# Moving the transpose of one bias out of a kernel's head, and settling its instruction order anew with a dearer table load

## The chip, the cores and the metric

The kernel runs on one core of a Trainium2 chip. The metric is device time in microseconds (us). The span that a profile reports is the time from the first to the last instruction; the device time is about 2 us longer.

Engines, as the profile names them: PE is TensorE's matmuls and PEld its weight loads, DVE is VectorE, ACT is ScalarE, POOL is GpSimd. SP only issues transfers here. PSUM has eight banks, in which PE leaves its results.

## The reference, cut to what matters

Two linear-attention blocks A and two feed-forward blocks B in turn, on 2048 tokens of width 512, with a LayerNorm before each and a residual sum after each.

```python
def _A_ref(x, wqkv, wo):
    q, k, v = split(x @ wqkv)                          # 32 heads of 16
    phi = lambda t: jnp.where(t > 0, t + 1, jnp.exp(t)) + 1e-6
    kv  = einsum(phi(k), v);  z = sum(phi(k))
    return (phi(q) @ kv) / (phi(q) @ z + 1e-6) @ wo
def _B_ref(x, w1, b1, w2, b2):
    h = gelu(layernorm(x) @ w1 + b1)                   # 512 -> 1792
    return h @ w2 + b2
x = x + _A_ref(layernorm(x), ...);  x = x + _B_ref(layernorm(x), ...)   # this line twice
```

The exponentials and logarithms of A and the Gelu of B need different ACT function tables, so ACT must load a table whenever it goes from one to the other.

## The kernel before

The kernel does not write its instructions in the order in which they run. It states a graph of operations. A small planner inside the program (a list scheduler) then simulates the engines with fixed costs, and from that settles, once and for all, the order on each engine and the PSUM bank of each tile. On the chip each engine follows its order strictly and waits on semaphores for what it needs. The planner's costs therefore cost no time on the chip; they only decide the order.

```python
SEM_LAT = 70.0
MM = 216.0
TABLE_LOAD = 1300.0        # what the planner thinks a table switch costs, in ns
...
                    if o.table is not None and table is not None and o.table != table:
                        at = max(o.ready, t0 + TABLE_LOAD)
                        pr += self.table_penalty
...
CONF = dict(N_HALF=1, N_K=4, ..., N_H=3, ..., TABLE_PENALTY=20.26, WINDOW=164.24,
            SHIFT={"B00_0": 1.5, "B00_1": -18.1, ...})   # priorities, found by search
```

`N_K` and `N_H` say how many PSUM banks the K products and the first feed-forward products may hold at once. `SHIFT` moves the priority of a group of operations.

The bias b1 (1792 numbers) is needed as a column for each block of 128. It is loaded as 14 rows, transposed by one small matmul and copied by ACT. In the kernel before that is planned ahead of everything but the warm-up matmuls:

```python
        b1b = Tile(psum, "b1", "g")
        G.op("pe", lambda e: e.matmul(bank(b1b)[:, 0:FT], lhsT=b1r[:, :], rhs=idp[0:FT, 0:FT], ...), 200,
             reads=["b1r", f"id{P}"], writes=["b1p"], tiles=[b1b], prio=-60, name="b1T", ...)
        G.op("act", lambda e: e.activation(b1c[:], bank(b1b)[:, 0:FT], ACT.Copy), 200, ..., prio=-60, name="b1c")
```

Two more operations: one is the LayerNorm of a tile of 128 tokens, whose inverse deviation comes from a chain of tiny POOL operations and which is then applied by DVE or ACT. The other is POOL's addition of b2 to the same tile:

```python
            G.op("dve", lambda e: e.tensor_scalar(yb[...], src(), mv[...], rstd[...],
                 op0=ALU.subtract, op1=ALU.mult), ..., name=f"norm{tag}", fast=True)
...
            G.op("pool", lambda e: e.tensor_tensor(xsb[:, st, :], xsb[:, st, :], b2b[:], op=ALU.add), 1120,
                 ..., prio=prio + 8, name=f"b2{L}_{st}")
```

## Time and profile before

| what | before |
|---|---|
| device time, median (range) | 344.92 us (344.75 to 345.35) |
| span of the profiled run | 343.1 us |
| PE, ACT, DVE, POOL busy | 96%, 72%, 58%, 31% |
| ACT table switches | 27, of 1283 ns each |
| first K matmul | at 10.04 us, waiting for its weights |

The first lines are from the page of before: busy time of each engine with its share of the span, and then the chain of work that ended last, by engine and by line.

```profile
PE 330.1 (96%) x1763; PEld 162.2 (47%) x1796; DVE 198.9 (58%) x430; ACT 247.6 (72%) x407; POOL 105.4 (31%) x199
...
PE 68%; ACT 12%; DVE 9%; POOL 5%; DMA 2%; issue 2%; ACTq 0%; DVEq 0%
...
L926 ACT ACT_TABLE_LOAD x27 | 34.6, 1283 | 0.5
```

PE is the limit, yet only 68% of the chain runs over PE. PE busy says little here, because the recorded matmuls overlap: one K product's matmul is recorded with a median of 379 ns, while in a stream the starts of full 128x512 matmuls are 216 ns apart. The spacing of the starts says more. I call every start that comes later than its predecessor's own time a stall.

These are PE's longest waits in before, from the waits view (what waited, for what, us in total, how often, longest; cut where dots stand):

```profile
PE ps L560 <- DVE yb L537: 1.6, 2, 1.0
...
PE ps L814 <- DMA b1r<-in_B_b_dram: 1.4, 1, 1.4
PE ps L599 <- DMA wqkv<-in_A_wqkv_dram: 1.1, 1, 1.1
PE ps L777 <- ACT t L570: 0.7, 1, 0.7
...
```

And this is the head in the timeline of before (start, duration, engine, line, operation, count, idle time before it and what ended it). L814 is the b1 matmul, L560 the transposes of the first tiles, L599 the first K product:

```profile
7.79 0.19 PE L814 MATMUL ps<-idp,b1r 14*128 14x14 bf16 x1 [1.41 <-DMA b1r<-in_B_b_dram]
7.91 1.03 PE L560 MATMUL ps<-idp,yb 128*128 128x128 bf16 x8
10.04 1.87 PE L599 MATMUL ps<-wqkv,t 128*128 128x512 bf16 x4 [1.09 <-DMA wqkv<-in_A_wqkv_dram]
```

PE waits 1.4 us for b1 and then does the transposes, but the K product behind them waits for its weights anyway.

### The profile page before, as it was taken

Reading aid. Unit: us, or ns where it says so; the run is one execution under the profiler, and the core shown is the slowest. Engines: PE = TensorE matmul, PEld = TensorE weight load, DVE = VectorE, ACT = ScalarE, POOL = GpSimd, SP = SyncE. Lnnn points to the kernel's source line nnn. Section 1 sums busy time; section 2 is a strip of 40 time slices with the busy share of each in tenths; the row PEclk is TensorE's granted clock in tenths of the full one; section 3 lists DMA queues with packets and bytes.
Section 4 is the critical chain, followed back from the end, with each engine's and each line's share of the span. In section 5 each row is a group of like instructions: output and inputs, shape, how many; then the busy total and the mean of one; then the engine's idle time right before and its main releaser. Section 6 shows DMA issues by size and latency. Waiting matters only on the chain.

```text
span 343.1 us, 4823 instructions
## 1 busy us (share of the span) xinstructions
PE 330.1 (96%) x1763; PEld 162.2 (47%) x1796; DVE 198.9 (58%) x430; ACT 247.6 (72%) x407; POOL 105.4 (31%) x199
## 2 busy tenths in 40 slices
PE   6899998999999999999999999998999999999996
PEld 2344453746544444444444454447744444444442
DVE  5588759759595343880375779989549218110122
ACT  1589669999979989968823399999995996527000
POOL 4662503526518031460022200054706604400000
PEclk9999999999999999999999999999999999999999
DMA  5832490004203020030011010000203301200011
GB/s 170 291 91 32 116 358 4 2 0 48 46 1 64 15 46 2 15 76 17 0 32 31 15 32 2 1 2 0 32 31 78 48 0 40 54 31 0 32 42 50
DMA packets 32116, 16.71 MB, mean 49 GB/s; under 512 B 26652, under 2 KB 30876, under 8 KB 32092
## 3 DMA queue, kind: packets, MB, share of 16 engines
q1 hardware_dynamic: 28876, 8.79, 12.6%
q0 software_dynamic: 1344, 5.77, 4.9%
q10 hardware_dynamic: 1872, 1.84, 1.6%
q8 instruction: 14, 0.23, 0.3%
q14 instruction: 10, 0.08, 0.1%
HBM read 8.00 MB, written 2.10 MB: 29 GB/s over the span
## 4 chain that ended last, share of the span: by engine, by line
PE 68%; ACT 12%; DVE 9%; POOL 5%; DMA 2%; issue 2%; ACTq 0%; DVEq 0%
PE ps L796 23%; PE ps L777 18%; PE ps L599 7%; PE ps L615 5%; PE ps L747 4%; ACT gT L783 4%; PE ps L680 4%; ACT L926 3%; PE ps L649 3%; DMA wqkv<-in_A_wqkv_dram 2%; DVE stats L513 2%; POOL xsb L763 2%; POOL rstd L525 2%; DVE xsb L752 2%; ACT eb L581 2%
## 5 line engine op out<-in xcount | busy, mean ns | idle before, releaser
L777 PE MATMUL ps<-t,w 128*128 128x512 bf16 (+1 forms) x555 | 102.0, 336 | 1.4 <-ACT t L570 0.7
L796 PE MATMUL ps<-w,gT 128*128 128x512 bf16 x441 | 101.4, 379 | 0.5
L783 ACT ACTIVATE gT<-ps,b1c 128x512 bf16<-128x512 f32 (+1 forms) x140 | 78.1, 605 | 21.4 <-PE ps L777 11.7
L777 PEld LDWEIGHTS ps<-t,w 128*128 128x128 bf16 x560 | 54.2, 98 | 45.8 <-ACT gT L783 2.1
L796 PEld LDWEIGHTS ps<-w,gT 128*128 128x128 bf16 x448 | 43.8, 98 | 52.2 <-ACT gT L783 0.5
L581 ACT ACTIVATE eb<-ps 128x512 bf16<-128x512 f32 x64 | 38.2, 598 | 22.6 <-PE ps L599 15.1
L763 POOL TENSOR_TENSOR xsb<-xsb,b2b 128x512 f32<-128x512 f32 x32 | 38.3, 1204 | 18.6 <-ACT yb L532 11.0
L585 DVE TENSOR_SCALAR eb<-eb 128x512 bf16<-128x512 bf16 x64 | 21.0, 329 | 39.4 <-ACT eb L581 39.4
L525 POOL TENSOR_TENSOR rstd<-veps,neghalf 128x1 f32<-128x1 f32 x64 | 37.2, 582 | 7.9 <-DVE veps L523 2.9
L583 ACT ACTIVATE rb<-ps 128x512 bf16<-128x512 f32 x64 | 38.4, 602 | 0.1
L734 DVE TENSOR_TENSOR t<-t,lr 128x512 bf16<-128x512 bf16 x32 | 22.4, 702 | 24.1 <-ACT lr L732 24.1
L806 DVE TENSOR_TENSOR outb<-ps,xsb 128x512 bf16<-128x512 f32 x16 | 11.1, 691 | 41.5 <-PE ps L796 41.5
L926 ACT ACT_TABLE_LOAD x27 | 34.6, 1283 | 0.5
L599 PE MATMUL ps<-wqkv,t 128*128 128x512 bf16 x124 | 32.6, 396 | 1.3 <-DMA wqkv<-in_A_wqkv_dram 1.1
L513 DVE BATCH_NORM_STATS2 stats<-xsb 128x6 f32<-128x512 f32 x48 | 32.8, 684 | 0.9
L747 PE MATMUL ps<-gtb,t 128*128 128x512 bf16 x124 | 31.5, 380 | 0.6 <-DVE t L734 0.2
L518 POOL TENSOR_SCALAR veps<-mv 128x1 f32<-128x1 f32 x32 | 6.3, 197 | 82.3 <-DVE mv L515 80.9
L615 PE MATMUL ps<-t,wqkv 128*128 128x512 bf16 x124 | 31.3, 379 | 0.2
L523 POOL TENSOR_SCALAR veps<-mv 128x1 f32<-128x1 f32 x29 | 8.1, 278 | 73.3 <-DVE mv L515 72.8
L532 ACT ACTIVATE yb<-xsb,nmr,rstd 128x512 bf16<-128x512 f32 x24 | 19.2, 809 | 13.1 <-PE ps L680 8.8
L537 DVE TENSOR_SCALAR yb<-xsb,mv,rstd 128x512 bf16<-128x512 f32 x24 | 18.4, 766 | 10.1 <-POOL rstd L525 9.7
L730 ACT ACTIVATE lr<-ps,eps 128x512 f32<-128x512 f32 x32 | 21.7, 679 | 1.7 <-PE ps L728 1.6
(59 smaller groups left out, 288.8 us busy)
## 6 DMA issues: line engine op xcount, KB each, us to landing
w<-in_B_w_dram POOLq DMA_DIRECT2D x4, 896.0 KB, 8.8
out_dram<-outb SPq DMA_DIRECT2D x16, 128.0 KB, 1.7
wqkv<-in_A_wqkv_dram ACTq DMA_DIRECT2D x2, 512.0 KB, 9.0
t<-in_A_x_dram POOLq DMA_DIRECT2D x2, 512.0 KB, 5.6
t<-yb SPq DMA_TRANSPOSE x48, 2.5
t<-in_A_x_dram ACTq DMA_DIRECT2D x1, 512.0 KB, 9.1
wqkv<-in_A_wqkv_dram POOLq DMA_DIRECT2D x1, 512.0 KB, 7.1
wo<-in_A_wo_dram POOLq DMA_DIRECT2D x1, 512.0 KB, 7.6
```

The lines of the kernel that those rows point to most:

```text
L513: G.op("dve", lambda e: e.bn_stats(stats[:, s.slot, :], src()), 620, reads=src_keys, writes=[k + "s"], tiles=[s, *src_tiles], prio=prio, n ...
L525: G.op("pool", lambda e: e.tensor_tensor(rstd[:, s.slot:s.slot + 1], veps[:, s.slot:s.slot + 1], neghalf[:], op=ALU.pow), 570, reads=[k + ...
L581: G.op("act", lambda e: e.activation(eb[:, et.slot, :], bank(bt), ACT.Exp), 478, reads=[src_key], writes=[f"e{tag}"], tiles=[bt, et], prio ...
L583: G.op("act", lambda e: e.activation(rb[:, rt.slot, :], bank(bt), ACT.Relu), 478, reads=[src_key], writes=[f"r{tag}"], tiles=[bt, rt], pri ...
L599: ins = e.matmul(bank(b), lhsT=yTa(yT)[:, dt, k * P:(k + 1) * P], rhs=wqkv[:, dt, D:2 * D], start=(dt == 0), stop=(dt == DT - 1))
L615: ins = e.matmul(bank(b), lhsT=wqkv[:, dt, kt * P:(kt + 1) * P], rhs=yTa(yT)[:, dt, :], start=(dt == 0), stop=(dt == DT - 1))
L747: ins = e.matmul(bank(wb), lhsT=yTa(pq)[:, kt, k * P:(k + 1) * P], rhs=gtb[:, kt, :], start=(kt == 0), stop=(kt == DT - 1))
L763: G.op("pool", lambda e: e.tensor_tensor(xsb[:, st, :], xsb[:, st, :], b2b[:], op=ALU.add), 1120, reads=[("x", st), "b2b"], writes=[("x", ...
L777: ins = e.matmul(bank(b, n), lhsT=w1[:, dt, ft * P:(ft + 1) * P], rhs=yTa(yT)[:, dt, k0 * P:k1 * P], start=(dt == 0), stop=(dt == DT - 1))
L783: G.op("act", lambda e, ft=ft, b=b, k0=k0, k1=k1, n=n: e.activation(gT[:, g.slot, ft * 512 + k0 * P:ft * 512 + k1 * P], bank(b, n), ACT.Ge ...
L796: ins = e.matmul(bank(b), lhsT=gT[:, g.slot, ft * 512 + k * P:ft * 512 + (k + 1) * P], rhs=w2[:, ft, :], start=(ft == 0), stop=(ft == FT - 1))
L926: e.preload_act_table_set(sets[table])
```

## The change

The intent: take b1's wait out of the head, and plan with 1420 ns for a table load instead of 1300, under which all the priorities were searched anew.

```diff
-TABLE_LOAD = 1300.0
+TABLE_LOAD = 1420.0
...
-    N_HALF=1, N_K=4, N_Q=2, P_Z0=8.53, ..., N_H=3, N_N=1, GAP=15.32,
-    TABLE_PENALTY=20.26, WINDOW=164.24,
+    N_HALF=1, N_K=1, N_Q=2, P_Z0=6.72, ..., N_H=4, N_N=1, GAP=17.68,
+    TABLE_PENALTY=30.47, WINDOW=138.33,
     SHIFT={                      # every entry replaced, cut here
...
-        b1b = Tile(psum, "b1", "g")          # ahead of the first stage
-        G.op("pe", ..., prio=-60, name="b1T", lat=MM_DRAIN)
-        G.op("act", ..., prio=-60, name="b1c")
...                                           # behind the first stage
+        G.grp = "b1"
+        b1b = Tile(psum, "b1", "g")
+        G.op("pe", ..., prio=-20, name="b1T", after=trs[-1:], lat=MM_DRAIN)
+        G.op("act", ..., prio=-20, name="b1c")
```

No arithmetic is added or removed. The order of all engines changes.

## The prediction

> **What bounds it now.** TensorE. The page's busy line gives PE 96% of the 343.1 us span, ACT 72%, DVE 58%. PE busy is no measure of its peak, so I took the spacing of matmul starts in the timeline: 216 ns for a full 128x512 matmul, 108 at half width, 55 for a 128-wide one. Holes of one matmul that recur every 10.8 us I take for missing records. Between the first K matmul (10.04 us) and the last matmul (340.2 us) about 8 us of stall is left: 1.9 us where matmuls run 427 ns apart (10.0 to 13.9 us); 0.75 at 16.8; 2.5 between 49 and 55 (KV chain between the stages); 0.85 at 61.3; 0.4 at 156; 0.6 at 217 to 220; 1.2 at 234; 0.5 at 258. The rest is matmul time, which the change leaves, a head of 10.0 us and a tail of 2.9 us. The wall time is 1.9 us above the span.
>
> **What the change does.**
> 1. *b1 out of the head.* In the timeline: one 14x14 matmul (0.19 us), its weight load (0.10), an ACT copy (0.18). The waits view shows PE idle 1.4 us on b1's DMA just before it, although the first normalised tile was ready at 5.5 us and warm-up ended near 6.4. Without it the first transposes start about 1.4 us earlier. But the chain of waits begins with the load of wqkv (1.72 to 9.90 us), on which the first K matmul waits. So that 1.4 us is off the critical path: first K matmul still at 10.0, at most 0.4 us saved behind it. The POOL loads that wait for the first transposed tile go out up to 1.9 us earlier and may delay wqkv or chunk 1 by tenths. At the end of stage one the same work costs PE 0.1 and ACT 0.2 us, off the KV chain.
> 2. *Dearer table load.* The Trainium skill, "ScalarE: Activation LUTs", section "What ACT_TABLE_LOAD costs", gives about 1283 ns plus a drain of about 1380. The trace has 1283 ns for all 27 switches and 1311 to 1313 ns from work to work in 26 of them: no drain. So 1300 was right; 1420 plans 27 x 0.108 = 2.9 us of slack for ACT. I expect fewer switches (22 to 27). ACT is 85 to 99% busy between 60 and 150 us, but PE loses under 1.5 us there, so ACT time saved is worth little.
> 3. *New order* (K banks 4 to 1, h banks 3 to 4, all shifts): no work added or removed; it can only move the 8 us of stall.
>
> **Sum.** With every stall gone the time would be near 337, just past 2% faster. The two barriers (49 to 62, 217 to 235 us) and the slow first matmuls are largely structural. The Trainium skill, "TensorE: Matmul & The Clock Gate", Part 1, has the full clock after about 3.4 us of sustained work in a free-running window; the trace agrees in kind (full rate 3.9 us after 10.04, though warm-up ran 4.9 us). With b1's wait gone, transposes follow warm-up directly and the full rate could come earlier: up to 1.9 us, weighed at a third. I expect 1 to 3 us less stall: 343.0 us, 340.0 to 346.0.
>
> **What would show it.** Right: first K matmul within 0.3 us of 10.0, no b1 wait in PE's waits, ACT_TABLE_LOAD still 1283 ns, stall sum 5 to 8 us. Wrong: first K matmul past 10.5 (DMA collision); ACT waiting on the one K bank, or PE idle for h banks, over 1 us in the waits; new stalls at the stage borders.
>
> Chances: faster by over 2% 0.04, within 2% 0.93, slower 0.03.

## More of the kernel before

In the middle of the kernel the chain leaves PE. Two pieces of the chain of before between 100 and 160 us (its shares by line, cut, and then pieces in order of time):

```profile
by line: ACT gT L783 22.9%; ACT L926 19.2%; POOL rstd L525 6.7%; ACT eb L581 5.8%; POOL xsb L763 5.7%; PE ps L777 5.7%; ACT rb L583 5.7%; issue 4.4%; DVE stats L513 4.3%; ACT yb L532 3.9%; POOL veps L523 3.0%; ACT lr L732 2.1%; ACT lr L730 
...
105.43 1.73 ACT gT L783 x3
107.18 1.28 ACT L926
108.47 0.60 ACT eb L581
109.07 0.49 ACT rb L583
109.58 1.28 ACT L926
```

Three Gelus (L783), a table load (L926), an exponential and a Relu, and a table load back. In this stretch the chain runs over ACT, and 19% of it is table loads. PE's stalls there are still small, so ACT and PE run neck and neck.

## The result

| what | before | after |
|---|---|---|
| device time, median (range) | 344.92 us (344.75 to 345.35) | 342.22 us (342.14 to 342.77) |
| span of the profiled run | 343.1 us | 340.0 us |
| ACT table switches | 27 | 21 |
| ACT busy between 100 and 160 us | 53.3 us | 41.2 us |
| first K matmul in this profile | 10.04 us | 9.12 us |

The ratio is 0.9923, with a 95% interval of 0.9906 to 0.9940. Ratios here are the mean time of one kernel's fast runs over that of the other's of the same rounds, so not quite the ratio of the medians quoted. The change is real and is 2.7 us, 0.8%: inside the range, and within 2%. Where I turn a ratio below into microseconds, I multiply its distance from 1 by 345.

The same views of after. The page first:

```profile
PE 328.6 (97%) x1764; PEld 162.1 (48%) x1796; DVE 196.5 (58%) x430; ACT 240.1 (71%) x401; POOL 106.7 (31%) x199
...
PE 89%; ACT 4%; DMA 2%; DVE 2%; issue 1%; POOL 1%; ACTq 0%
...
L928 ACT ACT_TABLE_LOAD x21 | 26.9, 1283 | 0.4
```

The chain is now 89% PE. PE's waits in after:

```profile
PE ps L600 <- DMA wqkv<-in_A_wqkv_dram: 1.6, 1, 1.6
...
PE ps L561 <- DVE yb L538: 1.2, 3, 0.7
PE ps L717 <- DVE kvb L713: 0.9, 1, 0.9
PE ps L600 <- ACT eb L582: 0.7, 1, 0.7
...
```

The b1 wait is gone, the wait for the weights has grown by 0.5 us, and there is a new one of 0.7 us, a K product that waits for the exponential that frees the one K bank. The head of after:

```profile
6.08 0.39 PE L561 MATMUL ps<-idp,yb 128*128 128x128 bf16 x4
7.14 0.40 PE L561 MATMUL ps<-idp,yb 128*128 128x128 bf16 x4 [0.67 <-DVE yb L538]
9.12 1.65 PE L600 MATMUL ps<-wqkv,t 128*128 128x512 bf16 x4 [1.59 <-DMA wqkv<-in_A_wqkv_dram]
```

And the chain of after between 100 and 160 us, its shares by line:

```profile
by line: PE ps L797 38.7%; PE ps L778 35.4%; PE ps L600 11.5%; PE ps L748 7.1%; PE ps L681 5.8%; PE ps L729 1.4%; issue 0.4%
```

Only matmuls are left there. The engines' busy time in the same 60 us, in the windows view (PE, PEld, DVE, ACT, POOL, each with its count of instructions; then the granted clock, the DMA share and GB/s), first before:

```profile
100.00:160.00 60.00, 59.30 (x269) 26.23 (x273) 32.32 (x67) 53.34 (x77) 23.98 (x46) 1.00 0.17 33
```

then after:

```profile
100.00:160.00 60.00, 59.74 (x275) 27.20 (x279) 34.97 (x71) 41.22 (x59) 23.54 (x46) 1.00 0.18 34
```

ACT's load in this stretch fell from 53.3 to 41.2 us: 7 table loads in it instead of 10, and other ACT work went elsewhere.

### Where the 2.7 us went

This table adds up PE's stalls of more than 60 ns by stretch. Some profiles miss a few per cent of the matmul records, so it uses two profiles that miss none and that differ from before and after only in where b1 stands in the head (runs `b_b1_late` and `a_b1_head` below). The border between the first and second stage lies at 45 to 65 us, that between the layers at 205 to 240 us.

| stretch, us | before's order | after's order | difference |
|---|---|---|---|
| 14.9 to 45 | 1.01 | 1.21 | +0.20 |
| 45 to 65 | 2.45 | 1.64 | -0.81 |
| 65 to 100 | 0.23 | 0.10 | -0.13 |
| 100 to 205 | 1.24 | 0.00 | -1.24 |
| 205 to 240 | 1.57 | 1.30 | -0.27 |
| from 240 | 0.47 | 0.00 | -0.47 |
| sum | 6.97 | 4.25 | -2.72 |

The difference of the stalls behind the head is as large as the whole gain. The head, then, should give nothing, although after's profile shows its first K matmul 0.92 us earlier. That contradiction is the first thing tested.

The planner's own simulation is of interest here. It ends at 336.7 us for before and 336.5 us for after: by its own reckoning the new order was worth 0.2 us. The chip ended its spans 6.4 and 3.5 us later than planned. So the new order is hardly a better plan; it is one that the chip can keep better. The planner has no stall over 0.1 us for before between 100 and 205 us, where the chip has 1.24 us.

### The profile page after: what moved, and what is told of

The parts are those of the page before. It is cut to its first block, busy times and chain, and to the rows that moved or that the text cites. A ratio compares the mean times of both kernels' runs of the same rounds, so it can differ in the third digit from the quotient of the medians.

```text
span 340.0 us, 4820 instructions
## 1 busy us (share of the span) xinstructions
PE 328.6 (97%) x1764; PEld 162.1 (48%) x1796; DVE 196.5 (58%) x430; ACT 240.1 (71%) x401; POOL 106.7 (31%) x199
## 4 chain that ended last, share of the span: by engine, by line
PE 89%; ACT 4%; DMA 2%; DVE 2%; issue 1%; POOL 1%; ACTq 0%
PE ps L778 28%; PE ps L797 28%; PE ps L600 8%; PE ps L748 7%; PE ps L616 6%; PE ps L681 4%; PE ps L650 3%; DMA wqkv<-in_A_wqkv_dram 2%; PE ps L729 2%; ACT eb L582 1%; PE ps L631 1%; PE ps L561 1%; ACT gtb L662 1%; ACT lr L731 1%; ACT lr L733 1%
## 5 line engine op out<-in xcount | busy, mean ns | idle before, releaser
L784 ACT ACTIVATE gT<-ps,b1c 128x512 bf16<-128x512 f32 (+1 forms) x140 | 78.9, 604 | 23.4 <-PE ps L797 12.8
L526 POOL TENSOR_TENSOR rstd<-veps,neghalf 128x1 f32<-128x1 f32 x64 | 38.3, 599 | 7.9 <-DVE veps L524 3.0
L600 PE MATMUL ps<-wqkv,t 128*128 128x512 bf16 x125 | 33.7, 393 | 2.8 <-DMA wqkv<-in_A_wqkv_dram 1.6
L586 DVE TENSOR_SCALAR eb<-eb 128x512 bf16<-128x512 bf16 x64 | 19.9, 317 | 25.6 <-ACT eb L582 25.2
L748 PE MATMUL ps<-gtb,t 128*128 128x512 bf16 x125 | 32.3, 379 | 0.6 <-ACT gtb L662 0.3
L928 ACT ACT_TABLE_LOAD x21 | 26.9, 1283 | 0.4
L538 DVE TENSOR_SCALAR yb<-xsb,mv,rstd 128x512 bf16<-128x512 f32 x24 | 16.4, 685 | 14.2 <-POOL rstd L526 14.0
```

The source lines that it names most:

```text
L526: G.op("pool", lambda e: e.tensor_tensor(rstd[:, s.slot:s.slot + 1], veps[:, s.slot:s.slot + 1], neghalf[:], op=ALU.pow), 570, reads=[k + ...
L600: ins = e.matmul(bank(b), lhsT=yTa(yT)[:, dt, k * P:(k + 1) * P], rhs=wqkv[:, dt, D:2 * D], start=(dt == 0), stop=(dt == DT - 1))
L748: ins = e.matmul(bank(wb), lhsT=yTa(pq)[:, kt, k * P:(k + 1) * P], rhs=gtb[:, kt, :], start=(kt == 0), stop=(kt == DT - 1))
L784: G.op("act", lambda e, ft=ft, b=b, k0=k0, k1=k1, n=n: e.activation(gT[:, g.slot, ft * 512 + k0 * P:ft * 512 + k1 * P], bank(b, n), ACT.Ge ...
L928: e.preload_act_table_set(sets[table])
```

## The experiments

Twelve kernels, all compared with before in five rounds. The names start with b where the kernel before was edited and with a where it was after. "Theory A" is that ACT had no slack in the old order between 100 and 290 us and has it in the new one. Its rivals are B (b1's wait), C (table loads cost time in any order, so six fewer are the gain), D (the constant itself makes the gain) and E (a collision of DVE and POOL). In the edits the planner runs as usual and its finished order is then changed by hand, unless stated otherwise; so all else keeps its place.

### Was it b1?

`b_b1_late`, correct result:

```diff
         order = sch.run()
+        for e, o, n in (("pe", b1T, "PTA0_1"), ("act", b1k, "tcA0_1")):
+            order[e].remove(o)                      # b1 behind the first two transposes
+            order[e].insert([q.name for q in order[e]].index(n) + 1, o)
```

> The kernel before, every engine's order as it was, only the b1 matmul and its copy moved behind the transposes and copies of the first two tiles. Theory A (the gain is made by slack on ACT between 100 and 290 us, the head gives at most a little): first transposes near 6.1 us, and the time is between 344.0 and 345.0 us. Rival B (waiting for b1 costs most of the gain): 342.0 to 343.5 us. In both, if the early landing of wqkv (8.98 us after, 9.90 before) follows from the b1 move, the first K matmul is at 9.1 us here; if it is chance or has another cause, it is at 10.0.

`a_b1_head`, correct result (the operation takes the warm-up's PSUM bank, and the waits that this needs are set anew):

```diff
         order = sch.run()
+        b1b.slot = wu.slot
+        for e, o, at in (("pe", b1T, order["pe"].index(wm) + 1), ("act", b1k, 0)):
+            order[e].remove(o)                      # b1 back in front of the transposes
+            order[e].insert(next(i for i, q in enumerate(order[e]) if i >= at and q.sem is None), o)
```

> The kernel after, order as it is, only the b1 matmul and its copy put back behind warm-up and ahead of the first transposes. Theory A: 342.2 to 343.2 us, so at least two thirds of the gain of 2.7 us stays. Rival B: 344 to 345 us. If the b1 wait is what delays the first K matmul it goes from 9.1 to about 10.0 us.

Measured: `b_b1_late` 345.57 us, ratio 1.0010 (0.9991 to 1.0028). `a_b1_head` 342.70 us, ratio 0.9927 (0.9905 to 0.9949), against 0.9923 for after. Moving b1 gives nothing to before, and putting it back takes nothing from after. Rival B is out.

The timeline of `b_b1_late` shows why:

```profile
5.85 0.39 PE L560 MATMUL ps<-idp,yb 128*128 128x128 bf16 x4
6.99 0.40 PE L560 MATMUL ps<-idp,yb 128*128 128x128 bf16 x4 [0.75 <-DVE yb L537]
7.32 0.18 PE L814 MATMUL ps<-idp,b1r 14*128 14x14 bf16 x1
9.92 1.87 PE L599 MATMUL ps<-wqkv,t 128*128 128x512 bf16 x4 [2.42 <-DMA wqkv<-in_A_wqkv_dram]
```

The transposes start 2 us earlier than in before, and PE then waits 2.4 us instead of 1.1 us for the weights. In `a_b1_head`, with b1 in front, the first K matmul came at 10.70 us. Over the 13 fast profiles it came between 9.12 and 10.70 us, in both kernels and in no relation to b1, although the load was always issued at 1.72 or 1.73 us. So the 0.92 us in the two profiles of the result was chance: after's was the earliest of all. b1's own landing varies too. It held PE for 1.4 us in before's profile; in that of `a_b1_head` the b1 matmul started at 6.32 us, as soon as warm-up was over.

### Was it the table loads?

`b_noswitch` and `a_noswitch`, wrong results: one function of the exponential's table stands in for Gelu, so that no load is needed. The trace confirms that the operation itself takes the same time (a median of 687 ns, against 681 with Gelu).

```diff
-   bank(b, n), ACT.Gelu_apprx_tanh, bias=b1c[:, ft:ft + 1], scale=1.0),
+   bank(b, n), ACT.Identity, bias=b1c[:, ft:ft + 1], scale=1.0),
...
-                if o.table is not None and o.table != table:
+                if False:                           # no table load
```

> Wrong result on purpose: the kernel before with Gelu replaced by Identity, so that none of the 27 table loads is needed; orders and all other work the same. Theory A (ACT has no slack in this order, and table loads push PE late from 100 us on): the time falls by 2 to 3 us, to 342 to 343 us, and PE's stalls at 111, 114, 126, 135, 156, 234 and 258 us are gone. Rival B (ACT is off the path): falls by less than 0.7 us.

> Wrong result on purpose: the kernel after with Gelu replaced by Identity, no table loads (21 fewer). Theory A (this order already has the slack): falls by less than 0.8 us, to 341.4 to 342.2 us. Rival C (table loads cost time in any order, and after is faster because it has six fewer, 7.7 us of ACT): falls by 2 us or more.

Measured: `b_noswitch` 344.12 us, ratio 0.9966 (0.9949 to 0.9984), a gain of 1.2 us (among runs of the same mean granted clock, the share of TensorE's full clock that the profile records, it is 1.4 us, four against three, and 1.6 us, two against seven; see the section on the clock). `a_noswitch` 341.66 us, ratio 0.9910 (0.9886 to 0.9933), 0.4 us below after's own ratio, with overlapping intervals. The old order gains from free table loads about what it lost between 100 and 205 us, or a little more: its stalls there went from 1.24 to 0.09 us, and the chain there is that of after:

```profile
by line: PE ps L777 52.9%; PE ps L796 27.7%; PE ps L599 8.6%; PE ps L747 6.6%; PE ps L615 2.9%; PE ps L728 1.4%
```

So theory A is right about that stretch and wrong about the rest: I had expected 2 to 3 us, and that the stalls at 234 and 258 us would vanish too. They stayed, at 1.13 and 0.47 us. Rival C is out, since 21 free loads gave after 0.4 us where C asked for 2 or more.

`b_dose` and `a_dose`, correct results: the opposite test, a little more ACT work at every table load.

```diff
                     e.preload_act_table_set(sets[table])
+                    e.activation(dose[:, turns:turns + 1], eps6[:], ACT.Copy)   # 128x1
+                    turns += 1
```

> The kernel before, orders the same, with one small ACT copy (128x1, about 0.19 us) added behind each of its 27 table loads: 5.1 us more on ACT. Theory A (its order has no slack on ACT): the time rises by 1.5 us or more, with new PE stalls between 100 and 170 us. Rival: under 0.7 us.

> The kernel after, orders the same, with the same small ACT copy behind each of its 21 table loads: 4.0 us more on ACT. Theory A (the 0.12 us planned too much for each load is slack): the time rises by less than 0.8 us, PE still without a stall over 0.3 us between 75 and 215 us. Rival C: it rises as much per load as the kernel before.

Measured: `b_dose` 346.56 us, ratio 1.0055 (1.0034 to 1.0077), 1.9 us slower. `a_dose` 342.36 us, ratio 0.9928 (0.9906 to 0.9951), as fast as after. This is the clearest result. PE's waits between 100 and 160 us in `b_dose`:

```profile
PE ps L778 <- ACT gT L784: 1.1, 3, 0.6
```

In before the same wait was 0.2 us in that window, and in `a_dose` the view lists no wait of PE there at all. The stalls between 100 and 205 us were 2.06 us in `b_dose` and 0.00 us in `a_dose`. The copies took 0.203 us each, so 4.3 us in all in the new order and 5.5 us in the old one. The new order takes them in with no loss that these runs can measure; the old one had little to spare: it lost 1.9 us when 5.5 us of copies were added.

### Was it the constant?

`b_t1420` and `a_t1300`, correct results. Here the planner settles the whole order anew:

```diff
-TABLE_LOAD = 1300.0        # b_t1420
+TABLE_LOAD = 1420.0
```

```diff
-TABLE_LOAD = 1420.0        # a_t1300
+TABLE_LOAD = 1300.0
```

> The kernel before with the planner's constant alone raised to 1420, the order settled anew with the old shifts; 25 loads. The planner's own end is 342.9 us against 336.7 for before. If the constant itself made the gain (theory D), this is faster than before. If only an order tuned under it does (theory A), this is slower, 346 to 349 us, but the chip ends at most 4 us after the plan's end, where before ends 6.4 us after it.

> The kernel after with the planner's constant alone put back to 1300, the order settled anew with the new shifts; 23 loads. The planner's own end is 341.2 us against 336.5 for after. Theory A: slower than after by 4 us or more, 346 to 349 us, and the chip ends 5 us or more after the plan (after: 3.5). Theory D: about the time of before, 345.

Measured: `b_t1420` 349.98 us, ratio 1.0155 (1.0136 to 1.0174). `a_t1300` 347.27 us, ratio 1.0074 (1.0057 to 1.0091). The constant alone does harm in both directions, so theory D is out: the shifts (125 in before, 127 in after) belong to the constant under which they were searched. Of my ranges, 346 to 349 us held for `a_t1300` and missed for `b_t1420`, and what I expected of the plans missed. Both ended later than planned by similar amounts (spans of 347.1 and 344.7 us, so 4.2 and 3.5 us after the plan's end), where I had expected `a_t1300` to slip by 5 us or more. So a plan made with 1300 does not always slip more than one made with 1420. That a search under 1420 leads to orders with slack is therefore plausible and not shown; shown is that this order has it.

### The stall at 234 us

It stayed without table loads, so it had another cause. These are the norms on DVE (L537) and the additions of b2 on POOL (L763) in before's timeline, with the transposes on PE behind the second norm:

```profile
228.42 1.15 POOL L763 TENSOR_TENSOR xsb<-xsb,b2b 128x512 f32<-128x512 f32 x1
228.64 1.22 DVE L537 TENSOR_SCALAR yb<-xsb,mv,rstd 128x512 bf16<-128x512 f32 x1
...
233.66 1.15 POOL L763 TENSOR_TENSOR xsb<-xsb,b2b 128x512 f32<-128x512 f32 x1
233.69 1.41 DVE L537 TENSOR_SCALAR yb<-xsb,mv,rstd 128x512 bf16<-128x512 f32 x1 [0.44 <-POOL rstd L525]
...
235.16 0.40 PE L560 MATMUL ps<-idp,yb 128*128 128x128 bf16 x4 [0.99 <-DVE yb L537]
```

And the corresponding norms of after:

```profile
222.64 0.53 DVE L538 TENSOR_SCALAR yb<-xsb,mv,rstd 128x512 bf16<-128x512 f32 x1
223.25 1.16 POOL L764 TENSOR_TENSOR xsb<-xsb,b2b 128x512 f32<-128x512 f32 x1 [1.03 <-DVE yb L538]
...
225.80 0.55 DVE L538 TENSOR_SCALAR yb<-xsb,mv,rstd 128x512 bf16<-128x512 f32 x1 [0.44 <-POOL rstd L526]
```

Both norms of before started beside an addition and ended 0.29 us behind its end; without a neighbour the norm takes 0.53 to 0.55 us. The Trainium skill, "SBUF — State Buffer", section "Who interferes with whom", says that POOL and some DVE instructions share a port pair that one holds for its whole instruction while the other blocks. These lines are consistent with it, and so are the others like them: seven norms of before started beside an addition, and each ended 0.28 or 0.29 us behind it. After is not free of such meetings: four of its norms took 1.37 to 1.42 us, but none of them cost PE a stall. The planner knows of it in part (the flag `fast`), but it had placed the second norm just ahead of the addition, and on the chip, some microseconds late, the two met.

`b_b2_moved`, correct result:

```diff
         order = sch.run()
+        at["b21_0"].deps[at["normB1_3"]] = True       # the additions wait for the last norm
+        for o in moved:                                # b21_0 to b21_3
+            order["pool"].remove(o)
+        i = order["pool"].index(at["powB1_3"]) + 1     # behind the norms' own POOL chain
+        order["pool"][i:i] = moved
```

> The kernel before, correct result, orders the same but for POOL: the four additions of b2 for the first chunk of the second layer go behind the chain of small POOL operations that the four layer norms need, and the first of them waits for the last norm. Before, the norms on DVE that ran beside such an addition took 1.2 and 1.4 us (0.53 us in after, where none ran beside), and PE stood still 1.16 us at 234 us. Theory E (this collision made that stall, and being free of it is part of what after gained): the stall at 234 us falls under 0.3 us and the time falls by 0.8 to 1.2 us, to 343.4 to 344.0. Rival: the stall stays over 0.8 us (ACT's table load or the transposed copy holds it).

Measured: 344.26 us, ratio 0.9973 (0.9950 to 0.9996), a gain of 0.9 us that is only just clear of noise: among runs of the same clock it is 1.4 us (three against eight) and 0.3 us (three against three). The profile is firmer: the stall at 234 us is down to 0.18 us, and the norms are at their own length again:

```profile
233.30 0.54 DVE L537 TENSOR_SCALAR yb<-xsb,mv,rstd 128x512 bf16<-128x512 f32 x1
233.93 2.72 POOL L763 TENSOR_TENSOR xsb<-xsb,b2b 128x512 f32<-128x512 f32 x2 [0.92 <-DVE yb L537]
```

The collision was a real cost of the old order. But the move helps the norm in a second way, by letting its POOL chain run ahead of the additions, and the run does not part the two. After has only a part of this gain: at the same border it keeps a stall of 0.54 us (at 226 us), because one addition still stands in front of a norm's POOL chain.

`b_both`, wrong result: `b_noswitch` and `b_b2_moved` in one.

> Wrong result on purpose: the kernel before with both causes taken away together, no table loads (Identity for Gelu) and the four b2 additions behind the norm chain. Alone they gave 1.2 and 0.9 us. If they are two separate causes they add: 342.5 to 343.2 us, a ratio to before of 0.993 to 0.995, so 1.7 to 2.4 of the 2.7 us that after gained, leaving the stalls at 258 us (0.47) and at 61 us (0.85), which after's order does not have, and which it trades for others between 41 and 57 us. If one hides the other: 343.4 us or more.

Measured: 342.37 us, ratio 0.9916 (0.9892 to 0.9941), a gain of 2.9 us where the two alone gave 2.1 us together, and I had expected at most 2.4. The excess goes with the clock (next section): five of the six runs here had a mean granted clock of 0.995, but only five of the 11 of before in the same rounds, which were spread from 344.03 to 346.83 us. Among these the gain is 2.2 us (five against five), within the range that I expected. So the two costs do add, within what the runs resolve. The old order without them is as fast as after. That does not mean that after gained at the same places: it has 1.24 us from the first, some 0.27 us at the second border, and the rest at the stage border and behind 240 us.

### The clock, and a version meant to beat both

`a_warm`, correct result: five more warm-up matmuls where PE stood idle in the head.

```diff
         order = sch.run()
+        fill(2, "fill1", "PTA0_1")      # ahead of the second transpose
+        fill(3, "fill2", "K0_0")        # ahead of the first K product
```

> The kernel after, correct result, with two spare warm-up matmuls between the first two transposes and three behind them, into the time in which PE stood idle. Tests the upside of the prediction, a full PE clock before the first K matmul. In the six profiles so far the matmuls behind the first K ran 427 ns apart for 3.3 to 5.9 us. If an unbroken run of matmuls from 1.5 us on brings the full rate before 10 us, the K matmuls run 216 ns apart from the first on and the time falls by 0.7 to 1.6 us, to 340.6 to 341.5. If the order behind is bound by DVE there, the stall at 16 us grows and the time falls by less than 0.5 us. If the rate stays at 427 ns, no change or up to 0.4 us slower.

Measured: five fast runs of 341.19 to 342.80 us, ratio 0.9906 (0.9890 to 0.9922), 0.6 us better than after's own ratio, with overlapping intervals. Their median, 341.50 us, lies at the edge of the 340.6 to 341.5 us expected for a full rate. One run, which was the profiled one, fell in a slow state: 389.55 us at a mean clock of 0.853. Its times are not used, and why a kernel on one core met this once is open. The mean granted clock was 0.999 or more in four of the five fast runs, and at most 0.995 in all four runs of after.

The profiles show what this number stands for. These are two stretches of the head of after in the windows view; the number behind the count of POOL is the granted clock:

```profile
6.00:7.00 1.00, 0.46 (x5) 0.21 (x3) 0.93 (x3) 0.50 (x1) 0.56 (x1) 1.00 0.73 230
...
10.00:11.00 1.00, 1.00 (x7) 0.59 (x6) 0.62 (x1) 0.20 (x1) 1.00 (x2) 0.50 0.95 357
```

After had the full clock from 5.96 us, before its first K matmul, and ran at half of it from 9.38 to 12.79 us. The spacing of the matmuls agrees: transposes start 56 ns apart at 6.1 us and 107 ns apart at 10.6 us. Of the 13 fast profiles 12 have clock records of the head. In each the full clock came, between 4.66 and 7.48 us; in all of them but that of `a_best` (below) it was halved 3.41 us later, for 3.41 us (seven profiles, mean clock 0.995) or for twice as long (four, mean clock 0.99). What decides between the two no run here shows. Before's own profile has no clock record ahead of 13.97 us, and the view counts that as full clock, although the matmuls there start 427 ns apart; so a mean of 1.00 is no proof by itself.

This matters for every comparison above. Of the 44 runs of before beside the experiments, 28 had a mean clock of 0.994 or 0.995 and took 344.6 us on average; 15 had 0.989 or 0.990 and took 345.6 us. A difference of less than 1 us between two kernels can therefore come from the mix of clocks. The main result does not: after's three runs at 0.995 took 342.2 us on average, 2.4 us below these runs of before at that clock (the clocks of before's four runs in the result itself are not on record). What `a_warm` gained goes with the clock: a mean of 0.999 or more became frequent, but it is no faster at 0.995 (one run, 342.80 us), and without the filler one run each of `a_b1_head` and `a_dose` had a mean clock of 1.0 and took 340.93 and 340.51 us.

`a_best`, correct result: `a_warm` with two edits for stalls that after has left.

```diff
+        order["dve"].insert(order["dve"].index(at["pr0_0_3"]), at["kvm0"])   # the KV mask earlier
+        for names, behind in ((("b21_1",), "nmrB1_0"), (("b21_3", "b21_0"), "nmrB1_2")):
+            ...                                                              # additions behind the norm chain
```

> A version meant to beat both, correct result: the kernel after with the five spare warm-up matmuls (alone 0.6 us faster than after), the mask of KV on DVE moved ahead of one product of the first chunk (stall at 56 us from 1.0 to about 0.5), and three b2 additions of the second layer's first chunk moved behind the norm chain (stall at 226 us from 0.54 to about 0.2). Theory: 340.4 to 341.2 us, ratio to before 0.986 to 0.989. If the freed time is lost again at the next wait: no faster than the warm-up alone, 341.5 us, ratio 0.990.

Measured: 341.68 us (341.23 to 342.35), ratio 0.9900 (0.9877 to 0.9923). It beats before by 1.0%. Its median is 0.5 us below that of after, with overlapping intervals of the ratios, so that it beats after is likely and not shown; it is no faster than the warm-up alone. Its profile tells of both edits. The one at the second border worked: the stalls of 205 to 240 us fell from 1.30 to 0.76 us. The one at the stage border was given back at the next wait. PE's waits of `a_best`:

```profile
PE ps L748 <- ACT gtb L662: 1.3, 1, 1.3
...
PE ps L717 <- DVE kvb L713: 0.4, 1, 0.4
```

The wait for the KV mask fell from 0.9 to 0.4 us, but the matmuls behind it now wait 1.3 us, instead of 0.3 us, for an ACT copy; the stretch from 45 to 65 us rose from 1.64 to 2.11 us. ACT had taken the logarithms and exponentials that the planner had put first. The full clock, granted at 4.97 us, was kept here to the last matmul. The first K matmuls, in the timeline of `a_best`:

```profile
10.11 1.02 PE L600 MATMUL ps<-wqkv,t 128*128 128x512 bf16 x4 [1.82 <-DMA wqkv<-in_A_wqkv_dram]
...
12.80 1.04 PE L600 MATMUL ps<-wqkv,t 128*128 128x512 bf16 x4 [0.58 <-ACT t L571]
```

Four K matmuls now take 1.02 us at the first attempt, where they took 1.87 us in before and 1.65 us in after.

## Why the prediction was right

The time (343.0 predicted, 342.22 measured) and the class were right, the size of the gain in part by luck: the one source of it that the prediction named, an earlier full clock, did not bring it, and the largest piece came from where it expected little. Point by point:

- *PE bounds the kernel, and only about 8 us of stall can move.* Right. All of the gain is found in PE's stalls: 6.97 us behind the head in the old order, 4.25 us in the new one.
- *The 1.4 us before b1 is off the critical path.* Right, and shown by two runs that moved b1 alone (ratio 1.0010, and 0.9927 against 0.9923).
- *The first K matmul stays within 0.3 us of 10.0.* Missed in after's profile (9.12 us), and a bad marker: it follows the landing of one load, which spread over 1.6 us from run to run. I had taken one profile's landing as a fixed time.
- *The table load has no drain, and 1300 was right.* The loads take 1283 ns in after too. From work to work 18 of its 21 took 1312 or 1313 ns; the three others waited for their input as well.
- *22 to 27 switches.* Just missed: 21.
- *ACT time saved is worth little.* This is the term that was mis-sized. The stalls of that stretch were indeed under 1.5 us, but they were the largest single piece of the gain, 1.24 of 2.72 us, and without table loads the old order is 1.2 us faster. I planned with the slack and gave it no worth; it was nearly half of the win.
- *The two barriers are largely structural.* Half right. The stage border gave 0.81 us and the layer border 0.27 us. That the second held a collision worth up to 0.9 us I had not seen, though the lengths of 1.2 and 1.4 us of its norms stood in the trace.
- *A full clock before 10 us, weighed at a third.* It came, at 5.96 us in after's profile, and was lost again at 9.38 us: the first K matmul still ran at the full rate, those behind it 427 ns apart until 12.7 us. The same happened in the old order with b1 in front (`b_dose`, `b_noswitch`), so b1 did not decide it. I had read the one profile whose clock records of the head are missing. With PE's idle time filled on purpose it lasted, in the profile of `a_best`; the filling brought about 0.6 us, with overlapping intervals.
- *A wait for the one K bank.* It appeared, 0.7 us, below the 1 us that would have counted against me.
- *New stalls at the stage borders*, named as a sign of being wrong. They did appear: after has one of 1.02 us at 56 us, on the KV mask. The border as a whole still lost less than before. The stalls from the first K matmul on add up to about 6.5 us in after's profile, inside the 5 to 8 us named as a sign of being right.

What stays open: the parts at the stage border (0.81 us) and behind 240 us (0.47 us) are read from traces and not tested by a run of their own; and whether the dearer constant as such led the search to an order with slack is not settled.

## What to carry to other kernels

A plan made ahead of time is worth what the machine can keep of it: two orders that the planner rated 0.2 us apart ran 2.7 us apart, and nearly half of that (1.24 us of stall) arose because one left its second-busiest engine a margin where that engine ran neck and neck with the first. Test for that margin directly by adding a little work to the suspected engine, here 0.2 us at each table load; the order without slack gave 1.9 us away and the other none. And before reading a difference from two profiles, look how far the same event wanders between profiles of one kernel: the 0.9 us by which the first real matmul came earlier was chance. Compare runs of the same mean clock, too: here it alone moved one kernel by 1 us.

## What the Trainium skill lacked or had wrong

- "ScalarE: Activation LUTs", section "What ACT_TABLE_LOAD costs": it adds a drain of about 1380 ns to each load of 1283 ns. The load is 1283 ns here as well, but in 26 of 27 switches of before the next ACT work began 1311 to 1313 ns after the work ahead of the load had ended; no drain shows.
- "TensorE: Matmul & The Clock Gate", Part 1: it has the full rate after about 3.4 us of sustained work and says that the point varies. In the 12 profiles with clock records of the head it came between 4.66 and 7.48 us, warm-up matmuls having begun at 1.51 us. What cost time here was its loss: in 11 of them the clock was halved 3.41 us after it came, for 3.41 or 6.83 us, although in after's profile PE's longest wait in that time was 1.6 us. The page also warns that clock records can't be trusted: before's own profile has none ahead of 13.97 us, so that the view shows a clock of 1.00 in a stretch in which its matmuls run 427 ns apart.
- "SBUF — State Buffer", section "Who interferes with whom": the runs are consistent with one blocking the other for a whole instruction, and add the cost for this pair, 1.22 and 1.41 us instead of 0.53 to 0.55 us for a 128x512 norm on DVE beside an addition on POOL.
- "DMA: Bandwidth & Descriptors": I found no figure there for how far the landing of one and the same load moves between runs. The 512 KB of K weights, issued at 1.72 or 1.73 us, let the first K matmul start between 9.12 and 10.70 us in 13 profiles.
